# Two gated layers after a spectral convolution: two weight slices on four tiles first, two groups by VectorE, outputs in two buffers

## Chip, cores and metric

The kernel runs on 1 core of one Trainium2 chip. The metric is the device time of one execution in microseconds (us). Each time is the median of several executions. One execution taken by the hardware profiler gives the trace.

## What is computed

```
X = rfft(x, axis=1);  y = irfft(X * (filt_r + 1j*filt_i), n=3008, axis=1)   # x: 2 x 3008 x 256
t = y.reshape(6016, 256)
t = (sigmoid(t @ w_gate) * (t @ w_val)) @ w_out          # d_ff 1536
h = t @ w_in2
out = (h * sigmoid(1.702 * h)) @ w_out2                  # d_ff 2048
```

The MLP weights arrive as float64 and are decoded on the chip.

## The kernel before

**Precision.** Each f32 operand of a layer is split in a rounded high part (ScalarE) and a low part (a subtraction on VectorE or GpSimd), tiles with names ending in 0 and 1. `mm3` multiplies in three passes: lines 120, 121 and 122 are high x high, weight high x input low, weight low x input high.

**Convolution.** `Conv` does a DFT of length 3008 in two factors, as matmuls against tables, in 8 groups of 32 channels with two halves each (16 steps), for one batch entry at a time. Steps a0 to d0 are batch 0, run alone at the start; a1 to e1 are batch 1, run between matmuls of the first layer. The last step, `d0`, leaves times in PSUM; VectorE transposes them to `tt` (L235), and `store` writes them to DRAM (`yscr`), where `load_y` fetches a tile later. Only for the layer's first two tiles of batch 0 do results go straight to their input `yraw`: by DMA out of `tt` (L243) for groups 0 to 6, by a second transpose on VectorE (L304) for group 7.

**First layer.** 12 tiles of 512 or 480 tokens. A *unit* (`s12`) is one tile with one of the 12 slices (f) of 128 hidden channels: 12 front matmuls (gate and value, two halves c of the input channels) into two of four PSUM banks ps0 to ps3, then `gated` (sigmoid on ScalarE L389, multiply on VectorE, split), then 6 back matmuls into the tile's accumulators (`s12_back`; ps4, ps5 or ps6, ps7). Backs run two units late (`push`, depth 2). Tiles 0 and 1 go first, slice by slice in turn, because the weights are still being decoded: `load_raw` brings 512 KB of float64 words (SP queue), `decode_steps` makes f32 of them with five VectorE passes (L153, L158, L161, L164, L168), one ScalarE pass, and a split with the low half on GpSimd (L117). There are 18 such pieces in the order `job_w1(0)`, `job_w2(0)`, `job_w1(1)`, ...; `job_w1(f)` is the gate and value slice f (`wg`), `job_w2(f)` two output slices (`wo`). For these two tiles `gated` works in place in PSUM, with the low half on VectorE (L392 multiply, L117 low half). Then tiles 2 to 11 follow, 12 units each; 40 of the units carry the convolution of batch 1. Results go to DRAM (`xscr`).

**Second layer.** Tiles in six pairs, with a seven-product scheme (Strassen-Winograd) over blocks of 2 x 2: `combine_w` makes sums of weights, `combine_x` of inputs; they are cut into `chores` that the loop calls at fixed places. Here the order on all engines is that of the code. A pair has 8 sets of 45 matmuls; after a pair its two output tiles are copied out of PSUM (L756, L758) into `o`, one buffer, and stored.

**Order.** SP runs its DMAs in the order of the code throughout. In the convolution and the first layer a scheduler places the other engines' instructions at build time; each engine then runs its list in order.

## Time and profile before

| | us |
|---|---|
| median of 3 runs (lowest, highest) | 1220.15 (1218.12, 1223.8) |
| the profiled execution | 1219.74 |
| its span in the trace | 1217.8 |
| TensorE matmuls busy | 1169.5 |
| VectorE / ScalarE / GpSimd busy | 681.5 / 659.0 / 573.4 |

The trace has, for each instruction, its start, duration and what released it. PE is TensorE, PEld its weight loads, DVE VectorE, ACT ScalarE, POOL GpSimd, SP the queue of most DMAs. A matmul of 512 columns shows about 0.39 us from start to end, but the next one starts sooner; so matmuls are counted against time, and a full bar does not mean full speed. A clock of 1.00 is 2.4 GHz, 0.50 is 1.2 GHz.

### The profile page before, as it was taken

Reading aid. Unit: us, or ns where it says so; the run is one execution under the profiler, and the core shown is the slowest. Engines: PE = TensorE matmul, PEld = TensorE weight load, DVE = VectorE, ACT = ScalarE, POOL = GpSimd, SP = SyncE. Lnnn points to the kernel's source line nnn. Section 1 sums busy time; section 2 is a strip of 40 time slices with the busy share of each in tenths; the row PEclk is TensorE's granted clock in tenths of the full one; section 3 lists DMA queues with packets and bytes.
Section 4 is the critical chain, followed back from the end, with each engine's and each line's share of the span. In section 5 each row is a group of like instructions: output and inputs, shape, how many; then the busy total and the mean of one; then the engine's idle time right before and its main releaser. Section 6 shows DMA issues by size and latency. Waiting matters only on the chain.

```text
span 1217.8 us, 14310 instructions
## 1 busy us (share of the span) xinstructions
PE 1169.5 (96%) x5072; PEld 951.0 (78%) x5072; DVE 681.5 (56%) x1055; ACT 659.0 (54%) x1171; POOL 573.4 (47%) x456
## 2 busy tenths in 40 slices
PE   8869899999999999999999989999999999999998
PEld 3447688887878888888888867878888888788886
DVE  7889944565553552452744547645546556555443
ACT  5445544565653443343433446666666666666664
POOL 6622314666653542433433334545545555455453
PEclk9979999999999999999999999999999999999999
DMA  7444501222202121120210110020010010200000
GB/s 183 117 153 131 129 1 60 53 74 68 71 14 79 51 87 52 35 87 15 72 35 1 52 52 1 1 70 1 1 70 1 25 44 1 70 1 1 35 1 33
DMA packets 31351, 61.73 MB, mean 51 GB/s; under 512 B 3088, under 2 KB 10512, under 8 KB 31280
## 3 DMA queue, kind: packets, MB, share of 16 engines
q1 hardware_dynamic: 30992, 60.57, 16.6%
q8 instruction: 39, 0.64, 0.2%
q10 hardware_dynamic: 288, 0.26, 0.1%
q14 instruction: 32, 0.26, 0.1%
HBM read 42.20 MB, written 17.69 MB: 49 GB/s over the span
## 4 chain that ended last, share of the span: by engine, by line
PE 85%; DVE 8%; issue 3%; DMA 2%; ACT 1%; POOL 1%; SPq 0%; ACTq 0%; DVEq 0%; POOLq 0%
PE ps L120 28%; PE ps L122 28%; PE ps L121 28%; DMA out_dram<-o 1%; DVE m L161 1%; DVE c L164 1%; PE ps L257 1%; DVE m L158 1%; DVE m L168 1%; DVE g L117 1%; DVE ps L392 0%; DVE yp L495 0%; DMA f<-in_fd_dram 0%; DVE y L282 0%; DVE z L292 0%
## 5 line engine op out<-in xcount | busy, mean ns | idle before, releaser
L117 POOL TENSOR_TENSOR g<-sg,g 128x512 fp32r<-128x512 f32 (+1 forms) x216 | 282.2, 1311 | 396.1 <-ACT g L116 383.2
L120 PE MATMUL ps<-yp,wg 128*128 128x512 f32 (+1 forms) x576 | 225.4, 391 | 14.5 <-ACT yp L116 7.8
L121 PE MATMUL ps<-yp,wg 128*128 128x512 f32 (+1 forms) x576 | 224.2, 389 | 4.3 <-POOL yp L117 4.3
L122 PE MATMUL ps<-yp,wg 128*128 128x512 f32 (+1 forms) x576 | 223.6, 388 | 0.0
L116 ACT ACTIVATE g<-sg 128x512 fp32r<-128x512 f32 (+1 forms) x216 | 134.6, 623 | 123.2 <-DVE sg L395 111.1
L742 DVE TENSOR_TENSOR sg<-ps,sg 128x512 f32<-128x512 f32 (+1 forms) x192 | 130.0, 677 | 114.9 <-ACT sg L739 109.0
L739 ACT ACTIVATE sg<-ps 128x512 f32<-128x512 f32 (+1 forms) x192 | 113.2, 590 | 140.9 <-DVE ps L818 42.8
L117 POOL TENSOR_TENSOR wo<-sg,wo 128x512 fp32r<-128x512 f32 (+1 forms) x96 | 126.3, 1326 | 116.4 <-ACT wo L116 102.6
L395 DVE TENSOR_TENSOR sg<-ps,sg 128x512 f32<-128x512 f32 (+1 forms) x120 | 80.8, 674 | 158.0 <-PE ps L122 151.1
L120 PEld LDWEIGHTS ps<-yp,wg 128*128 128x128 f32 x576 | 109.0, 189 | 39.1 <-DVE g L117 9.9
L389 ACT ACTIVATE sg<-ps 128x512 f32<-128x512 f32 (+1 forms) x144 | 84.1, 584 | 89.6 <-POOL g L117 47.2
L121 PEld LDWEIGHTS ps<-yp,wg 128*128 128x128 f32 x576 | 109.0, 189 | 25.3 <-POOL yp L117 5.2
L122 PEld LDWEIGHTS ps<-yp,wg 128*128 128x128 f32 x576 | 108.9, 189 | 21.0
L122 PE MATMUL ps<-g,wo 128*128 128x512 f32 (+1 forms) x288 | 111.7, 388 | 0.0
L121 PE MATMUL ps<-g,wo 128*128 128x512 f32 (+1 forms) x288 | 111.6, 388 | 0.0
L120 PE MATMUL ps<-g,wo 128*128 128x512 f32 (+1 forms) x288 | 111.6, 388 | 0.0
L120 PE MATMUL ps<-g,wp 128*128 128x512 f32 (+1 forms) x192 | 74.8, 390 | 6.4 <-ACT o L756 6.4
L120 PE MATMUL ps<-wg,wi 128*128 128x512 f32 (+1 forms) x192 | 74.1, 386 | 0.8 <-DVE ps L822 0.8
L122 PE MATMUL ps<-g,wp 128*128 128x512 f32 (+1 forms) x192 | 74.3, 387 | 0.0
L121 PE MATMUL ps<-g,wp 128*128 128x512 f32 (+1 forms) x192 | 74.2, 387 | 0.0
L121 PE MATMUL ps<-wo,wp 128*128 128x512 f32 (+1 forms) x192 | 74.1, 386 | 0.0
L122 PE MATMUL ps<-wo,wp 128*128 128x512 f32 (+1 forms) x192 | 74.1, 386 | 0.0
(152 smaller groups left out, 2192.1 us busy)
## 6 DMA issues: line engine op xcount, KB each, us to landing
raw<-in_w_out_dram SPq DMA_DIRECT2D x14, 512.0 KB, 3.8
f<-in_fd_dram SPq DMA_DIRECT2D x16, 384.0 KB, 4.7
xscr<-x SPq DMA_DIRECT2D x12, 512.0 KB, 3.2
yraw<-xscr SPq DMA_DIRECT2D x12, 512.0 KB, 4.9
x<-in_xd_dram SPq DMA_DIRECT2D x15, 384.0 KB, 4.6
yscr<-tt SPq DMA_DIRECT2D x40, 128.0 KB, 2.2
yraw<-yscr SPq DMA_DIRECT2D x10, 512.0 KB, 5.4
raw<-in_w_in_dram SPq DMA_DIRECT2D x8, 512.0 KB, 3.6
```

Source lines behind the costliest of these rows:

```text
L116: nc.scalar.activation(out=dst_hi, in_=src, func=AF.Copy)
L117: lo_eng.tensor_sub(dst_lo, src, dst_hi.bitcast(F32))
L120: nc.tensor.matmul(out=o, lhsT=w[0], rhs=x[0], start=first, stop=False, **kw)
L121: nc.tensor.matmul(out=o, lhsT=w[0], rhs=x[1], start=False, stop=False, **kw)
L122: nc.tensor.matmul(out=o, lhsT=w[1], rhs=x[0], start=False, stop=last, **kw)
L158: nc.vector.tensor_scalar(m, hw, 0xFFFFF, 0x100000, op0=ALU.bitwise_and, op1=ALU.bitwise_or)
L161: nc.vector.scalar_tensor_tensor(out=f, in0=lw, scalar=2.0**-32, in1=m, op0=ALU.mult, op1=ALU.add)
L164: nc.vector.scalar_tensor_tensor(out=cu, in0=hw, scalar=0x80000000, in1=cu, op0=ALU.bitwise_and, op1=ALU.bitwise_or)
L389: nc.scalar.activation(out=sg[:, :n], in_=sig_src[:, :n], func=AF.Sigmoid, scale=scale)
L395: nc.vector.tensor_mul(sg[:, :n], val_src[:, :n], sg[:, :n])
L739: nc.scalar.activation(out=self.sg, in_=self.bank, func=AF.Sigmoid, scale=1.702)
L742: nc.vector.tensor_mul(self.sg, self.bank, self.sg)
```

## The change

1. **Convolution.** Groups 6 and 7 of batch 0 are transposed by VectorE straight into `yraw`; their DMAs out of `tt` fall away.
2. **First layer.** After slices 0 and 1 on tiles 0 and 1, slices 0 and 1 (`FK = 2`) run on tiles 2 and 3, too; then tiles 0 and 1 go on with slices 2 to 11, and later tiles 2 and 3 with slices 2 to 11 (10 units each). Since the accumulators are needed again, the partial sums of all four tiles are copied by ScalarE to new tiles `part` and stored in `xscr`; before the last back matmuls they are loaded again and added by VectorE in place of the copies. Tile 3's input is split once more later, after a second load.
3. **Staging.** Raw weights go alternately through two pools of one buffer each (before: one pool with three raw buffers).
4. **Loads of tile 6.** In tile 5 the load comes at slice 8 and the split at slice 10 (before 3 and 8).
5. **Second layer.** Output tiles use the two `yraw` buffers in place of the one `o`; for the last pair the first half's DMA is issued from ScalarE's queue. `combine_w` is cut in five chores (before three), and the loop calls a fourth chore per set.

```
-            if b == 0 and g < 7:
+            if b == 0 and g < 6:
...
-            if g == 7:
+            if g >= 6:
                 nc.vector.transpose(
-                    yraw[u][96:, 1, :].rearrange("p (n c) -> p n c", c=32), ...
+                    yraw[u][g % 4 * 32:g % 4 * 32 + 32, 1, :].rearrange("p (n c) -> p n c", c=32), ...
...
+    FK = 2
+    part = {}
...
-        acc = accs[1 if t == 1 else 0]
+        acc = accs[t % 2 if t < 2 or (t < 4 and f < FK) else 0]
...
+            if f == FC1 - 2 and t < 4:
+                part[t] = new_raw()
+                nc.sync.dma_start(out=part[t], in_=xscr[t]...)
...
+            if f == FK - 1 and t < 4:
+                part[t] = hold.tile([P, 2, 512], F32, name=f"part{t}")
+                for c in range(2):
+                    nc.scalar.copy(part[t][:, c, :n], acc[c][:, :n])
+                nc.sync.dma_start(out=xscr[t]..., in_=part[t])
+            elif last:
+                if t < 4:
+                    x2 = part[t]
+                    for c in range(2):
+                        nc.vector.tensor_add(x2[:, c, :n], x2[:, c, :n], acc[c][:, :n])
...
-    stage[0] = pools.enter_context(tc.tile_pool(name="st1", bufs=2))
-    nraw[0] = 3
-    for _ in range(3):
+    stage.append(right.enter_context(tc.tile_pool(name="st1", bufs=1, side="right")))
+    for _ in range(2):
         next_raw()
...
-    raw = load_y(2)
-    for f in range(1, FC1):
+    raw = [load_y(2), load_y(3)]
+    for t in range(2):
+        s12(t, 1, parts[t], in_place=True)
...
+    for f in range(FK):
+        for t in (2, 3):
+            s12(t, f, parts[t], in_place=True)
+            if raws:
+                decode()
+                next_raw()
+    for f in range(FK, FC1):
         for t in range(2):
             s12(t, f, parts[t], in_place=True)
             if raws and (t == 0 or f % 2 == 1):
...
-        for f in range(FC1):
+        for f in range(FK if t < 4 else 0, FC1):
...
+        return [
+            whole,
+            lambda: sums(0),
+            lambda: (hi(0), hi(1), sums(1)),
+            lambda: (lo(0), lo(1), hi(2), hi(3)),
+            lambda: (lo(2), lo(3)),
+        ]
...
-                if f == 3 and t > 2:
+                if f == (8 if t == 5 else 3):
                     raw = load_y(t + 1)
-                if f == 8:
+                if f == (10 if t == 5 else 8):
...
-                    outs[t] = work.tile([P, 2, 512], F32, tag="o", name="o", bufs=1)
+                    outs[t] = new_raw()
...
-                nc.sync.dma_start(out=out[...], in_=outs[t][:, c, :n])
+                (nc.scalar if t >= nt - 2 and c == 0 else nc.sync).dma_start(out=out[...], in_=o)
...
             bx.sig()
             back()
+            chore()
```

How the built programs stand, at three places. First VectorE, right after the last transposes of the convolution of batch 0. `ex`, `m`, `c` belong to decoding, `sg` and `g` to the gating of tiles 0 and 1 (PSUM banks ps1 and ps3). Before:

```order
L235 STREAM_TRANSPOSE tt_495<-ps7_78 96x512
L153 TENSOR_SCALAR ex_527<-raw_447 128x512
L158 TENSOR_SCALAR m_531<-raw_447 128x512
L161 SCALAR_TENSOR_TENSOR m_531<-raw_447,m_531 128x512
L164 SCALAR_TENSOR_TENSOR c_529<-raw_447,c_529 128x512
L153 TENSOR_SCALAR ex_553<-raw_449 128x512
L168 SCALAR_TENSOR_TENSOR m_531<-m_531,c_529 128x512
L158 TENSOR_SCALAR m_557<-raw_449 128x512
L164 SCALAR_TENSOR_TENSOR c_555<-raw_449,c_555 128x512
L161 SCALAR_TENSOR_TENSOR m_557<-raw_449,m_557 128x512
L153 TENSOR_SCALAR ex_594<-raw_452 128x512
L168 SCALAR_TENSOR_TENSOR m_557<-m_557,c_555 128x512
```

Now:

```order
L237 STREAM_TRANSPOSE tt_491<-ps7_78 96x512
L394 TENSOR_TENSOR ps1_72<-ps1_72,sg_521 128x512
L155 TENSOR_SCALAR ex_528<-raw_446 128x512
L160 TENSOR_SCALAR m_532<-raw_446 128x512
L394 TENSOR_TENSOR ps3_74<-ps3_74,sg_548 128x512
L117 TENSOR_TENSOR g1_524<-ps1_72,g0_523 128x512
L163 SCALAR_TENSOR_TENSOR m_532<-raw_446,m_532 128x512
L166 SCALAR_TENSOR_TENSOR c_530<-raw_446,c_530 128x512
L117 TENSOR_TENSOR g1_551<-ps3_74,g0_550 128x512
L170 SCALAR_TENSOR_TENSOR m_532<-m_532,c_530 128x512
L155 TENSOR_SCALAR ex_555<-raw_448 128x512
```

Three decodings stood ahead of the first gating multiply (the third is shown only in part); now both multiplies and both low halves (`g1`) are mixed with the first decoding.

TensorE at the same place: `wg` times `yp` is front, `wo` times `g` is back. Before, from the end of the first slice on:

```order
L122 MATMUL ps3_74<-yp0_124,wg1_82 128x512
L120 MATMUL ps0_71<-yp0_122,wg0_81 128x512
L121 MATMUL ps0_71<-yp1_123,wg0_81 128x512
L122 MATMUL ps0_71<-yp0_122,wg1_82 128x512
L120 MATMUL ps0_71<-yp0_122,wg0_81 128x512
L121 MATMUL ps0_71<-yp1_123,wg0_81 128x512
L122 MATMUL ps0_71<-yp0_122,wg1_82 128x512
```

Now:

```order
L122 MATMUL ps3_74<-yp0_124,wg1_82 128x512
L120 MATMUL ps4_75<-g0_523,wo0_83 128x512
L121 MATMUL ps4_75<-g1_524,wo0_83 128x512
L122 MATMUL ps4_75<-g0_523,wo1_84 128x512
L120 MATMUL ps5_76<-g0_523,wo0_83 128x512
L121 MATMUL ps5_76<-g1_524,wo0_83 128x512
L122 MATMUL ps5_76<-g0_523,wo1_84 128x512
L120 MATMUL ps0_71<-yp0_122,wg0_81 128x512
L121 MATMUL ps0_71<-yp1_123,wg0_81 128x512
```

The back of tile 0's first slice (it needs the first piece of `wo`) has moved ahead of the second slice's front matmuls.

Last VectorE in the second layer's first pair, between the multiply of one set and the first addition of the next (L807, now L852). `wv` and `wr` are sums of weights, the rows that write `wi1` and `yp1` their low halves. Before:

```order
L742 TENSOR_TENSOR sg_5575<-ps3_74,sg_5575 128x512
L495 TENSOR_TENSOR wi1_3086<-wr_5517,wi0_3085 128x128
L495 TENSOR_TENSOR yp1_5122<-wr_5517,yp0_5121 128x128
L495 TENSOR_TENSOR yp1_5503<-wr_5517,yp0_5502 128x128 x2
L742 TENSOR_TENSOR sg_5590<-ps0_71,sg_5590 128x512
L483 TENSOR_TENSOR wv_5592<-wi0_3085,wi1_3086 128x512
L484 TENSOR_TENSOR wr_5593<-wv_5592 128x128
L485 TENSOR_TENSOR wr_5593<-wr_5593,wv_5592 128x128
L486 TENSOR_TENSOR wr_5593<-wv_5592 128x128
L487 TENSOR_TENSOR wr_5593<-wv_5592,wr_5593 128x128
L807 TENSOR_TENSOR ps2_73<-ps2_73,s15_5512 128x512
```

Now:

```order
L783 TENSOR_TENSOR sg_5601<-ps3_74,sg_5601 128x512
L511 TENSOR_TENSOR wr_5549<-wv_5548 128x128
L512 TENSOR_TENSOR wr_5549<-wv_5548,wr_5549 128x128
L518 TENSOR_TENSOR wi1_3218<-wr_5549,wi0_3217 128x128
L518 TENSOR_TENSOR yp1_5154<-wr_5549,yp0_5153 128x128
L783 TENSOR_TENSOR sg_5616<-ps0_71,sg_5616 128x512
L518 TENSOR_TENSOR yp1_5535<-wr_5549,yp0_5534 128x128 x2
L852 TENSOR_TENSOR ps2_73<-ps2_73,s15_5544 128x512
```

The row `wv` and two of the sums have gone behind the addition or ahead of this piece.

## Rows read from the trace of the kernel before

**Rows 1.** The page, part 4: the ending chain, share of the span by engine.
```profile
PE 85%; DVE 8%; issue 3%; DMA 2%; ACT 1%; POOL 1%; SPq 0%; ACTq 0%; DVEq 0%; POOLq 0%
```

**Rows 2.** Waits of TensorE, whole span: releaser, us in total, times, longest.
```profile
PE ps L120 <- DVE g L117: 6.5, 6, 3.4
PE ps L120 <- ACT o L756: 6.4, 5, 1.3
PE ps L120 <- ACT s L812: 5.7, 2, 3.6
```

**Rows 3.** Stretches: busy us (instructions) of PE, PEld, DVE, ACT, POOL; granted clock, DMA.
```profile
75.20:78.80 3.60, 0.79 (x1) 0.29 (x1) 2.44 (x4) 3.00 (x4) 3.60 (x3) 0.50 0.66 224
78.80:84.90 6.10, 6.07 (x15) 4.83 (x16) 5.37 (x6) 2.16 (x4) 3.48 (x3) 0.52 0.48 145
84.90:113.90 29.00, 29.00 (x129) 23.99 (x128) 28.33 (x45) 15.75 (x28) 7.00 (x6) 1.00 0.35 115
113.90:147.00 33.10, 29.79 (x124) 22.46 (x123) 33.10 (x53) 15.73 (x27) 9.24 (x7) 1.00 0.51 138
147.00:160.00 13.00, 9.62 (x36) 7.45 (x35) 9.29 (x12) 9.41 (x16) 9.36 (x7) 0.87 0.07 14
```

**Rows 4.** Timeline after the first convolution: start, us, engine, line; [idle before, releaser].
```profile
65.44 1.16 SPq L243 DMA_DIRECT2D yraw<-tt  x2
...
66.60 1.57 DVE L304 STREAM_TRANSPOSE yraw<-ps 32x512 f32<-32x512 f32 x2 [0.59 <-PE ps L299]
...
74.71 2.85 POOL L117 TENSOR_TENSOR wo<-m,wo 128x512 fp32r<-128x512 f32 x1 [13.11 <-ACT wo L116]
...
75.20 0.79 PE L120 MATMUL ps<-yp,wg 128*128 128x512 f32 x1 [7.78 <-ACT yp L116]
...
78.83 0.80 PE L121 MATMUL ps<-yp,wg 128*128 128x512 f32 x1 [2.83 <-POOL yp L117]
...
83.68 0.63 PE L120 MATMUL ps<-yp,wg 128*128 128x512 f32 x1
```

**Rows 5.** Timeline of VectorE, first layer's first two tiles.
```profile
91.33 0.69 DVE L392 TENSOR_TENSOR ps<-ps,sg 128x512 f32<-128x512 f32 x1
...
103.29 1.73 DVE L161 SCALAR_TENSOR_TENSOR m<-raw,m 128x512 f32<-128x512 uint32 x1
...
146.83 0.69 DVE L392 TENSOR_TENSOR ps<-ps,sg 128x512 f32<-128x512 f32 x1
...
163.14 0.70 DVE L392 TENSOR_TENSOR ps<-ps,sg 128x512 f32<-128x512 f32 x1 [2.02 <-PE ps L122]
...
167.22 0.70 DVE L392 TENSOR_TENSOR ps<-ps,sg 128x512 f32<-128x512 f32 x1 [2.02 <-PE ps L122]
```

**Rows 6.** Timeline of TensorE, where decoding ends.
```profile
151.57 0.50 PE L120 MATMUL ps<-yp,wg 128*128 128x512 f32 x1 [3.38 <-DVE g L117]
```

**Rows 7.** Timeline of the second layer's first pair of tiles.
```profile
719.05 2.89 DVE L495 TENSOR_TENSOR yp<-wr,yp 128x128 fp32r<-128x128 f32 x3
...
723.50 1.24 DVE L485 TENSOR_TENSOR wr<-wr,wv 128x128 f32<-128x128 f32 x1
...
725.06 0.69 DVE L807 TENSOR_TENSOR ps<-ps,s 128x512 f32<-128x512 f32 x1
...
726.97 0.79 PE L120 MATMUL ps<-wg,yp 128*128 128x512 f32 x1 [3.64 <-ACT s L812]
```

**Rows 8.** Timelines of the first pair boundary and of the end.
```profile
809.22 0.58 ACT L756 COPY o<-ps 128x512 f32<-128x512 f32 x1 [1.40 <-DMA out_dram<-o]
...
809.86 0.50 PE L120 MATMUL ps<-g,wp 128*128 128x512 f32 x1 [1.31 <-ACT o L756]
...
1211.83 0.38 PE L122 MATMUL ps<-wo,wp 128*128 128x480 f32 x1
...
1213.73 0.66 DVE L758 COPY o<-ps 128x480 f32<-128x480 f32 x1 [2.13 <-DMA out_dram<-o]
```

**Rows 9.** The page, part 6: DMA issues of one kind, KB, median us to landing.
```profile
raw<-in_w_out_dram SPq DMA_DIRECT2D x14, 512.0 KB, 3.8
```

More of the change, by code (lines that the diff above doesn't have):

```diff
@@ L127 @@
     ebias = const.tile([P, 1], F32, name="ebias")
-    stage = [None]
-    nraw = [1]
+    stage = []
+    turn = [0]
     raws = []
@@ L133, in load_raw @@
         dst, srcs, shape = job
-        raw = stage[0].tile([P, 512, 2], U32, tag="raw", name="raw", bufs=nraw[0])
+        st = stage[turn[0] % len(stage)]
+        turn[0] += 1
+        raw = st.tile([P, 512, 2], U32, tag="raw", name="raw")
         at = 0
@@ L142, in load_raw @@
             at += n
-        raws.append((raw, dst, shape))
+        raws.append((raw, dst, shape, st))
     def decode(lo_eng=None):
@@ L149, in decode_steps @@
     def decode_steps(lo_eng=None):
-        raw, dst, shape = raws.pop(0)
+        raw, dst, shape, st = raws.pop(0)
         lw, hw = raw[:, :, 0], raw[:, :, 1]
-        ex = stage[0].tile([P, 512], U32, tag="ex", name="ex")
+        ex = st.tile([P, 512], U32, tag="ex", name="ex")
         nc.vector.tensor_single_scalar(ex, hw, 0x7FF00000, op=ALU.bitwise_and)
         yield
-        c = stage[0].tile([P, 512], I32, tag="c", name="c")
+        c = st.tile([P, 512], I32, tag="c", name="c")
         nc.scalar.activation(out=c, in_=ex, func=AF.Relu, bias=ebias, scale=8.0)
-        m = stage[0].tile([P, 512], U32, tag="m", name="m")
+        m = st.tile([P, 512], U32, tag="m", name="m")
         nc.vector.tensor_scalar(m, hw, 0xFFFFF, 0x100000, op0=ALU.bitwise_and, op1=ALU.bitwise_or)
@@ L430, in s12_mm @@
         mm3(o[:, :n], [w[:, f, v, c, :] for w in wg], [y[:, c, :n] for y in yp], c == 0, c == 1)
+    FK = 2
+    part = {}
     def s12_back(t, f, gp):
         n = tiles[t][3]
-        acc = accs[1 if t == 1 else 0]
+        acc = accs[t % 2 if t < 2 or (t < 4 and f < FK) else 0]
+        first, last = f == 0, f == FC1 - 1
+        if t < 4:
+            first, last = f in (0, FK), f in (FK - 1, FC1 - 1)
         def back():
+            if f == FC1 - 2 and t < 4:
+                part[t] = new_raw()
+                nc.sync.dma_start(out=part[t], in_=xscr[t].rearrange("(c p) n -> p c n", p=P))
             for c in range(2):
                 cs = slice(c * P, (c + 1) * P)
-                mm3(acc[c][:, :n], [w[:, f, cs] for w in wo], gp, f == 0, f == FC1 - 1)
-            if f == FC1 - 1:
-                x2 = work.tile([P, 2, 512], F32, tag="o", name="x2", bufs=1)
-                nc.scalar.copy(x2[:, 0, :n], acc[0][:, :n])
-                nc.vector.tensor_copy(x2[:, 1, :n], acc[1][:, :n])
+                mm3(acc[c][:, :n], [w[:, f, cs] for w in wo], gp, first, last)
+            if f == FK - 1 and t < 4:
+                part[t] = hold.tile([P, 2, 512], F32, name=f"part{t}")
+                for c in range(2):
+                    nc.scalar.copy(part[t][:, c, :n], acc[c][:, :n])
+                nc.sync.dma_start(out=xscr[t].rearrange("(c p) n -> p c n", p=P), in_=part[t])
+            elif last:
+                if t < 4:
+                    x2 = part[t]
+                    for c in range(2):
+                        nc.vector.tensor_add(x2[:, c, :n], x2[:, c, :n], acc[c][:, :n])
+                else:
+                    x2 = work.tile([P, 2, 512], F32, tag="o", name="x2", bufs=1)
+                    nc.scalar.copy(x2[:, 0, :n], acc[0][:, :n])
+                    nc.vector.tensor_copy(x2[:, 1, :n], acc[1][:, :n])
                 if n < 512:
@@ L541 @@
     conv = Conv(0, early.enter_context(tc.tile_pool(name="fx0", bufs=3)), ff0, fw0)
-    stage[0] = early.enter_context(tc.tile_pool(name="st0", bufs=1))
+    right = ExitStack()
+    stage.append(right.enter_context(tc.tile_pool(name="st0", bufs=1, side="right")))
     nc.scalar.dma_start(out=tabs[:, :256], in_=tab[:, :256])
@@ L606 @@
     split_y(1, yraw[1], parts[1], 1, nc.vector, slice(96, P))
+    pools.close()
+    pools = ExitStack()
+    hold = pools.enter_context(tc.tile_pool(name="hold", bufs=1))
     for t in range(2):
@@ L614 @@
         next_raw()
-    raw = load_y(2)
-    for f in range(1, FC1):
+    raw = [load_y(2), load_y(3)]
+    for t in range(2):
+        s12(t, 1, parts[t], in_place=True)
+    parts += [new_parts(), [hold.tile([P, 2, 512], F32R, name=f"yh{i}") for i in range(2)]]
+    for t in (2, 3):
+        for c in range(2):
+            split_y(t, raw[t - 2], parts[t], c)
+    for f in range(FK):
+        for t in (2, 3):
+            s12(t, f, parts[t], in_place=True)
+            if raws:
+                decode()
+                next_raw()
+    np_ = parts[2]
+    for f in range(FK, FC1):
         for t in range(2):
@@ L621 @@
                 next_raw()
-            if f == 2 and t == 0:
-                np_ = new_parts()
-                for c in range(2):
-                    split_y(2, raw, np_, c)
-                raw = load_y(3)
     while raws:
@@ L629 @@
     pools.close()
+    right.close()
+    stage.clear()
     pools = ExitStack()
@@ L684 @@
                     wp = [w34.tile([P, FC2, D], F32R, name=f"wp{i}") for i in range(2)]
-                    stage[0] = ctx.enter_context(tc.tile_pool(name="st2", bufs=1))
-                    nraw[0] = 1
+                    stage.append(ctx.enter_context(tc.tile_pool(name="st2", bufs=1)))
                     for i in range(0, FC2, 2):
```

36 lines of the change are left out of this document (20 added, 16 removed).

## The prediction

> **What bounds the kernel now.** I read the page first: the chain that ended last is TensorE for 85% of the span [rows 1], so only what makes TensorE stop, or run at its lower clock, can be won back. The waits of TensorE by releaser come next [rows 2]: three of the groups lie where the change works. VectorE's low half of the gated value (6.5 us in 6 waits) belongs to the first layer's first two tiles, the copy of an output tile (6.4 us in 5 waits) to the second layer's pair boundaries, the copy at L812 (5.7 us in 2) to its first pair. Two more waits are read in the stretch after the first convolution [rows 4]: 7.78 us until 75.20 for a high half and 2.83 us until 78.83 for a low half of the input.
>
> Then the stretches [rows 3], where the reader should set matmuls against time. From 84.9 to 113.9 us, 129 matmuls take 29.00 us, 0.225 each, though VectorE is already full. From 113.9 to 147.0 only 124 run in 33.1 us (27.9 at that pace), from 147.0 to 160.0 only 36 in 13.0 (8.1). These two lose 5.2 + 4.9 = 10.1 us. VectorE is why: while it decodes weights, its multiply of one unit (a pass of one weight slice over one tile, 12 + 6 matmuls) comes at 91.33 and, 11 units later, at 146.83, so 5.05 us per unit; without decoding the next two stand 4.08 apart [rows 5], which is TensorE's own pace. The last of these waits, 3.38 us, ends at 151.57 [rows 6].
>
> The profiled execution took 1219.74 us (span 1217.8), 0.4 under the median 1220.15. Savings are taken off it, and the 0.4 added back at the end.
>
> **The part after the first convolution.** Before, groups 4 to 6 of the convolution reach the tiles' second half of channels by DMA, the last issued at 65.44 [rows 4], and TensorE's next matmul waits until 75.20. Now groups 6 and 7 are written by VectorE. That adds two transposes of the kind that took 1.57 us for two [rows 4]; they stand ahead of the last convolution steps, so these end some 1 us later, near 69.0. ScalarE and VectorE then need two short passes each (about 0.65, estimated from the 0.69 of a multiply [rows 5]), and the 12 matmuls of the second half run at about 69 to 72 us instead of 75.20 to 83.68.
>
> Most of this is given back by the new order on VectorE. The two gating multiplies now stand ahead of the decoding of the next two weight pieces, and on TensorE the first six output matmuls ahead of the second slice. Counted from 71.7 us: two multiplies, two low halves and five steps of the first piece, about 0.6 apart, end at 76.6; ScalarE's high half and GpSimd's low half (0.6 and 1.3) make the output weights ready near 78.6. The second piece takes VectorE until about 80.2 (one step delayed by GpSimd) and is ready at 82.2. So the second slice starts at 82.3, against 83.68 before [rows 4], with six output matmuls behind it that before were still ahead. The wait of some 4 us before it drops the clock: after the 7.78 us wait the 6.1 us from 78.8 were run at 0.52, the 1.2 GHz level [rows 3]. I carry the same stretch over, until about 88. By 91.8 us TensorE has then done 48 matmuls of this layer, before 46. Worth **0.5 us**. Bounds: if GpSimd's pass again takes 2.85 us, as at 74.71 [rows 4], and pushes VectorE as much, 2.5 lost; if no clock is lost and nothing collides, 4.5 won.
>
> **The decode stretch.** Tiles 2 and 3 are taken in for the first two slices: four units more that need no new weights, so decoding gets 16.3 us more of TensorE work to hide behind (4 x 4.08 [rows 5]). These units come off the later stage, so the total of matmuls is unchanged. Price on VectorE: the 55.5 us between the two multiplies [rows 5] hold 11 units of two passes (2 x 0.69), two input splits (1.4) and 12 decodings, so one decoding is (55.5 - 15.2 - 1.4) / 12 = 3.24 us. In the new order 13 units in a row carry one decoding each: 1.38 + 3.24 = 4.62 us against 4.08, a lag of 0.54 per unit, 7.0 in all, behind a start about 0.9 late. The four front banks let TensorE run ahead by 30 matmuls (6.7 us) less the chain of four passes (2.6): 4.1 us. So 7.0 + 0.9 - 4.1 = 3.8 us of waits by this, and none if the passes pack as in the first 29 us of the stretch. I take 2.5 and keep 0 to 3.8: gain 10.1 - 2.5 = **7.6 us**.
>
> What comes with it: eight ScalarE copies, eight VectorE adds in place of four copies on each engine, four stores and four loads of 512 KB, and a second load of tile 3. ScalarE is busy 15.75 of 29.00 us in the densest stretch [rows 3]; the adds come when decoding is over. Zero, with this cover; without it each add would cost about 0.7. On SP the stores wait for ScalarE's copies, and the loads of raw weights stand behind them, with two raw buffers instead of three. A load of 512 KB lands after 3.8 us [rows 9], inside two decodings, so I count nothing; the fourth rival prices it. Tile 6 of the first layer is now loaded later in its predecessor; its split has about one unit of spare time, so 0 to 2 us.
>
> **Outputs through two buffers.** At each of five pair boundaries the second tile's copy waits for the first one's DMA (1.40 us at 809.22), TensorE 1.31 behind it [rows 8]. Two buffers take the wait away: **6.4 us** [rows 2]. They are shared with the inputs of the next combination, whose loads were queued behind these stores anyway. At the end the last copy starts at 1213.73 although the last matmul was issued at 1211.83 [rows 8] and takes 0.4: **1.5 us**. One output DMA of each last tile now goes from ScalarE's queue. The Trainium skill (DMA: Bandwidth & Descriptors, Issuing engines are not separate DMA queues) says that issuing from several engines saves only issue time. No run here shows that yet; by it this edit alone is worth under 1 us, and the sum does not count it.
>
> **Smaller combination steps.** In the first pair VectorE does four low halves (0.28 + 2.89 us), a multiply and five sums in a row before the addition at 725.06, and TensorE waits 3.64 us for it [rows 7]. Now at most two sums, a multiply and four short halves stand there: 2.4 us if GpSimd is quiet, 5.0 if each half costs what the three did, against 6.1. That takes 1.1 to 3.7 off the first wait and most off the second. Against it, two sums now precede another addition, 0.5 to 2.5 us. Range 0.7 to 7; I take **4 us**.
>
> **The sum.** 0.5 + 7.6 + 6.4 + 1.5 + 4 = 20.0: 1219.74 - 20.0 = 1199.7, and 1200 beside the median.
>
> **Rivals.** (1) VectorE stays the bound. At the old 5.05 us per unit over 13 units TensorE would lose 13 x 0.97 + 0.9 - 4.1 = 9.4 us and the stretch gives 0.7: 1207. For it: a step took 1.73 us at 103.29 where a multiply takes 0.69 [rows 5], while GpSimd worked. Against: this pace held 12 decodings and two splits in 11 units. The Trainium skill (SBUF — State Buffer, Who interferes with whom) calls the port that VectorE and GpSimd share an exclusive lock whose loser fully blocks; by that rule each unit pays such a meeting, which is this rival's time, and the trace agrees in the 1.04 us extra.
> (2) The start costs more: gating ahead of decoding, with GpSimd's 2.85 us pass [rows 4] met twice. The second slice starts 5 us later: 1205.
> (3) The start costs less: the clock holds and the copies collide little; with no lag in the stretch, 0.5 + 7.6 become 4.5 + 10.1 and the first pair gives 5: 1192.
> (4) Slower: SP's queue starves decoding. It decides when a decoding takes over 6.5 us: 13 x (6.5 - 4.08) + 0.9 - 4.1 = 28.3 us of waits against 22.5 at most won (20.0 + 2.5), 1226. With two buffers that needs 10 us from release to landing, against 3.8 [rows 9].
> (5) The second buffer does nothing, since the combination's inputs hold it: 6.4 less, 1206.
>
> **How the numbers follow.** Forecast 50%, (1) 17, (2) 11, (3) 13, (4) 4, (5) 5. 0.5% is 6.1 us, about what a measurement of this kernel tells from no change: faster than 1214 takes in all but (4) and bad sums of several, 0.93; within it 0.04; slower 0.03. The range takes in (1), (2), (3) and (5) with a little of their spread: 1191 to 1210.
>
> **What would show it.** Right: the first unit of tile 2 starts near 92 us; TensorE at 0.225 us per matmul from there past 150, with under 4 us of waits for the gated low half; no waits for the output copies; waits of the first pair under 3 us; VectorE's last copy right behind the last matmul. Wrong: VectorE waiting for raw weights, TensorE waiting for the first output weights beyond 79 us, or the clock at half past 90.

## The result, and the profile after

| | before | after |
|---|---|---|
| median (lowest, highest), us | 1221.89 (1218.12, 1223.8) | 1208.26 (1206.53, 1210.13) |
| ratio, 95% interval | | 0.9893 (0.9867 to 0.9919) |
| the profiled execution, its span | 1219.74, 1217.8 | 1206.53, 1204.7 |

Faster by 13.6 us; 20 were forecast. 1208 lies inside the range 1191 to 1210, near its upper end, 8 us above the forecast of 1200 and next to the time of the first rival, 1207.

Both programs issue 5072 matmuls, so the two traces can be set against each other by the start of the n-th one (counted from 0). What the difference (after less before) gains from one n to the next belongs to the stretch between. Two later executions with the same order on every engine, `after_again` and `split5` (below), stand beside it, since one execution has its own luck:

| matmuls | stretch | forecast | after | after_again | split5 |
|---|---|---|---|---|---|
| 0 to 48 | convolution, first groups | 0 | +2.4 | +1.8 | +0.1 |
| 48 to 176 | its end, and the start of layer 1 | -0.5 | -0.7 | +0.9 | -0.3 |
| 176 to 600 | decode stretch | -7.6 | -3.2 | -2.0 | -0.7 |
| 600 to 1600 | tiles 2 to 5, second convolution | 0 | +1.3 | +1.0 | -0.5 |
| 1600 to 2880 | rest of layer 1 | 0 | 0 | 0 | 0 |
| 2880 to 3040 | first pair of layer 2 | -4 | -4.3 | -4.4 | -4.4 |
| 3040 to 5071 | pair boundaries | -6.4 | -6.4 | -6.5 | -6.3 |
| behind the last matmul | end | -1.5 | -2.1 | -2.1 | -2.1 |
| sum | | -20.0 | -13.1 | -11.2 | -14.2 |

The second layer came as forecast in sum. In the profiled execution 7 us are missing: 4.4 in the decode stretch, 2.4 in the first groups of the convolution and 1.3 in tiles 2 to 5, less 1.1 that came on top in the other rows.

Waits of TensorE in the changed kernel (answering [rows 2]; releaser, us in total, times, longest):

```profile
PE ps L120 <- DVE g L117: 5.5, 6, 2.0
...
PE ps L120 <- DVE y L342: 2.7, 1, 2.7
PE ps L120 <- DVE ps L867: 2.2, 1, 2.2
...
PE ps L120 <- ACT s L857: 1.1, 1, 1.1
```

No wait for an output copy is left (6.4 before), and the first pair's 5.7 became 2.2 + 1.1. The wait for the gated low half only shrank from 6.5 to 5.5. The matmuls of some stretches (length, TensorE busy and count, granted clock, DMA share, GB/s):

```profile
80.00:100.00 20.00, 18.71 (x63) 0.76 0.30 95
100.00:120.00 20.00, 20.00 (x90) 1.00 0.61 193
120.00:140.00 20.00, 18.89 (x84) 1.00 0.46 149
140.00:160.00 20.00, 16.05 (x67) 1.00 0.44 137
160.00:180.00 20.00, 19.60 (x87) 1.00 0.42 101
```

TensorE runs 0.222 us per matmul only until 120; the loss begins later than before [rows 3], but it comes. The timeline of VectorE and SP shows why (start, us, engine, line; idle before and releaser in brackets):

```profile
98.92 0.68 DVE L170 SCALAR_TENSOR_TENSOR m<-m,c 128x512 f32<-128x512 f32 x1
...
101.16 0.70 DVE L394 TENSOR_TENSOR ps<-ps,sg 128x512 f32<-128x512 f32 x1 [0.80 <-ACT sg L391]
102.85 0.69 DVE L117 TENSOR_TENSOR g<-ps,g 128x512 fp32r<-128x512 f32 x1 [0.99 <-ACT g L116]
105.39 0.43 DVE L155 TENSOR_SCALAR ex<-raw 128x512 uint32<-128x512 uint32 x1 [1.85 <-DMA raw<-in_w_val_dram]
...
128.70 1.43 DVE L155 TENSOR_SCALAR ex<-raw 128x512 uint32<-128x512 uint32 x1 [0.88 <-DMA raw<-in_w_out_dram]
```
```profile
100.14 0.36 SPq L455 DMA_DIRECT2D xscr<-part  x1
100.60 0.41 SPq L140 DMA_DIRECT2D raw<-in_w_gate_dram  x1
101.06 0.87 SPq L140 DMA_DIRECT2D raw<-in_w_val_dram  x1
```

From 99.6 to 105.4 VectorE decodes nothing. In its list only the gating of two units stands there, for which it waits 0.80 and 0.99 us, and then raw weights are missing for 1.85 us more. After that it is full until 165, apart from 0.88 us before 128.70. The second thing to see is what GpSimd's low half of a decoded piece does to a VectorE step that begins beside it:

```profile
134.69 1.35 POOL L117 TENSOR_TENSOR wo<-m,wo 128x512 fp32r<-128x512 f32 x1 [4.83 <-ACT wo L116]
...
152.46 1.29 POOL L117 TENSOR_TENSOR wg<-m,wg 128x512 fp32r<-128x512 f32 x1 [3.77 <-ACT wg L116]
```
```profile
134.79 0.69 DVE L394 TENSOR_TENSOR ps<-ps,sg 128x512 f32<-128x512 f32 x1
...
152.57 1.72 DVE L163 SCALAR_TENSOR_TENSOR m<-raw,m 128x512 f32<-128x512 uint32 x1
```

The step at L163 takes 0.68 us alone; begun just behind GpSimd's pass it takes 1.72 and ends half a microsecond after that pass (153.75). The multiply L394, which reads PSUM, takes its 0.69 in the same place. Steps with one input are held, too: L155 at 128.70 takes 1.43 us in place of 0.42, GpSimd's pass having begun at 128.56. From 105 to 165 us twelve steps are held in this way, for 10.9 us in all.

### The profile page after: what moved, and what is told of

Same layout as the page of the kernel before. It is cut to its first block, busy times and chain, and to the rows that moved or that the text cites. A ratio compares the mean times of both kernels' runs of the same rounds, so it can differ in the third digit from the quotient of the medians.

```text
span 1204.7 us, 14326 instructions
## 1 busy us (share of the span) xinstructions
PE 1170.2 (97%) x5072; PEld 949.1 (79%) x5072; DVE 694.9 (58%) x1067; ACT 661.9 (55%) x1177; POOL 570.4 (47%) x452
## 4 chain that ended last, share of the span: by engine, by line
PE 87%; DVE 8%; issue 2%; DMA 2%; ACT 1%; POOL 0%; SPq 0%; DVEq 0%; ACTq 0%
PE ps L120 28%; PE ps L122 28%; PE ps L121 28%; DVE c L166 1%; DVE m L163 1%; DVE ps L394 1%; DVE m L170 1%; PE ps L259 1%; DVE m L160 1%; DVE g L117 1%; DVE y L284 0%; DVE ex L155 0%; DMA raw<-in_w_out_dram 0%; DVE z L294 0%; DVE a L261 0%
## 5 line engine op out<-in xcount | busy, mean ns | idle before, releaser
L117 POOL TENSOR_TENSOR g<-sg,g 128x512 fp32r<-128x512 f32 (+1 forms) x212 | 277.6, 1314 | 374.6 <-ACT g L116 353.9
L120 PE MATMUL ps<-yp,wg 128*128 128x512 f32 (+1 forms) x568 | 221.6, 391 | 6.1 <-DVE g L117 5.5
L121 PE MATMUL ps<-yp,wg 128*128 128x512 f32 (+1 forms) x568 | 220.6, 388 | 1.8 <-POOL yp L117 1.5
L122 PE MATMUL ps<-yp,wg 128*128 128x512 f32 (+1 forms) x568 | 220.3, 388 | 0.6 <-POOL wg L117 0.6
L116 ACT ACTIVATE g<-sg 128x512 fp32r<-128x512 f32 (+1 forms) x212 | 132.0, 623 | 111.5 <-DVE sg L397 100.9
L117 POOL TENSOR_TENSOR wo<-sg,wo 128x512 fp32r<-128x512 f32 (+1 forms) x96 | 130.0, 1364 | 111.4 <-ACT wo L116 91.6
L783 DVE TENSOR_TENSOR sg<-ps,sg 128x512 f32<-128x512 f32 (+1 forms) x192 | 129.9, 677 | 89.9 <-ACT sg L780 82.5
L397 DVE TENSOR_TENSOR sg<-ps,sg 128x512 f32<-128x512 f32 (+1 forms) x116 | 77.9, 671 | 150.7 <-PE ps L122 143.5
L120 PEld LDWEIGHTS ps<-yp,wg 128*128 128x128 f32 x568 | 107.3, 189 | 30.4 <-DVE g L117 8.3
L121 PEld LDWEIGHTS ps<-yp,wg 128*128 128x128 f32 x568 | 107.3, 189 | 22.3 <-POOL yp L117 1.8
L122 PEld LDWEIGHTS ps<-yp,wg 128*128 128x128 f32 x568 | 107.2, 189 | 21.9 <-POOL wg L117 1.4
L120 PE MATMUL ps<-wg,wi 128*128 128x512 f32 (+1 forms) x192 | 74.1, 386 | 2.2 <-DVE ps L867 2.2
L120 PE MATMUL ps<-g,wp 128*128 128x512 f32 (+1 forms) x192 | 74.3, 387 | 0.0
L122 PE MATMUL ps<-wo,wp 128*128 128x512 f32 (+1 forms) x192 | 74.1, 386 | 0.0
L121 PE MATMUL ps<-wo,wp 128*128 128x512 f32 (+1 forms) x192 | 74.1, 386 | 0.0
L121 PE MATMUL ps<-wg,wi 128*128 128x512 f32 (+1 forms) x192 | 74.1, 386 | 0.0
L120 PE MATMUL ps<-wo,wp 128*128 128x512 f32 (+1 forms) x192 | 74.1, 386 | 0.0
```

The costliest lines, as they stand in the source:

```text
L116: nc.scalar.activation(out=dst_hi, in_=src, func=AF.Copy)
L117: lo_eng.tensor_sub(dst_lo, src, dst_hi.bitcast(F32))
L120: nc.tensor.matmul(out=o, lhsT=w[0], rhs=x[0], start=first, stop=False, **kw)
L121: nc.tensor.matmul(out=o, lhsT=w[0], rhs=x[1], start=False, stop=False, **kw)
L122: nc.tensor.matmul(out=o, lhsT=w[1], rhs=x[0], start=False, stop=last, **kw)
L397: nc.vector.tensor_mul(sg[:, :n], val_src[:, :n], sg[:, :n])
```

## The experiments

The theories on the decode stretch: **A**, VectorE is starved of raw weights (by the stores in SP's queue, or by having two buffers); **B**, each decoding is dear because VectorE is held once per piece by GpSimd. Two more on tile 5: **D**, the input split beside GpSimd; **E**, the shifted convolution steps. All ratios are to the kernel before, timed beside each kernel on the same chip. "Stretch" is matmuls 176 to 600 by the count above.

### part_act

```
-                nc.sync.dma_start(out=xscr[t]..., in_=part[t])
+                nc.scalar.dma_start(out=xscr[t]..., in_=part[t])
```

> The changed kernel with one edit: the four stores of partial sums are issued from ScalarE's queue, so that on SP no load of raw weights stands behind a store that waits for ScalarE's copies. Theory A (starved decoding): in the changed kernel SP's next raw load waited behind the first such store from about 91.5 until 100.6 us, and VectorE decoded nothing between 99.5 and 105.4; this time is missing later, where TensorE waits 5.5 us in six waits for the gated low half. It expects VectorE to decode through that stretch, the six waits to shrink to 2 us or less in total, and about 3.5 us less than the changed kernel (1204 to 1205). Theory B (each decoding is dear because VectorE meets GpSimd's low half once per piece, 1.0 to 1.1 us each): the waits stay at 4 us or more and the time within 1.5 us of the changed kernel (1207 to 1209).

Measured: 1209.84 us, 0.9884 (0.9868 to 0.99); stretch -1.0. VectorE did decode through 99 to 105, and then starved later, so the stores in SP's queue are not what keeps TensorE waiting:

```profile
104.83 0.37 SPq L140 DMA_DIRECT2D raw<-in_w_out_dram  x1
```
```profile
104.13 0.68 DVE L166 SCALAR_TENSOR_TENSOR c<-raw,c 128x512 uint32<-128x512 uint32 x1
...
109.69 0.43 DVE L155 TENSOR_SCALAR ex<-raw 128x512 uint32<-128x512 uint32 x1 [2.95 <-DMA raw<-in_w_out_dram]
```
```profile
PE ps L120 <- DVE g L117: 6.7, 9, 1.1
```

The load goes out the moment the buffer is free (its last reader, L166, ends at 104.81) and VectorE gets on 4.9 us later. VectorE waited 4.9 us for raw weights in this stretch, 2.7 before the edit, and TensorE 6.7 us for the gated low half, 5.5 before.

### low_dve

```
             if raws:
-                decode()
+                decode(nc.vector)
...
             if raws and (t == 0 or f % 2 == 1):
-                decode()
+                decode(nc.vector)
...
     while raws:
-        decode()
+        decode(nc.vector)
```

> The changed kernel with one edit: from the first unit of tiles 2 and 3 on, the low half of each decoded weight piece is made by VectorE instead of GpSimd. GpSimd then does nothing in this stretch that VectorE could meet. Theory B (meetings): 13 pieces lose 1.04 us each and gain a pass of 0.60, so VectorE's price per unit falls from 4.97 (59.6 us for 12 units between 105.4 and 165.0) to 1.20 + 2.46 + 0.60 = 4.26, the waits of TensorE for the gated low half fall from 5.5 to under 1 us, and the time by 4 to 5 us (1203 to 1204). No pass of 0.42 us or 0.69 us should show 1.4 to 1.8 us any more. Theory A alone (the 5 us without raw weights is the whole loss): the gap of VectorE before 105.4 us stays, the price per unit matters little, and TensorE still waits 3 us or more. Rival C: the extra pass waits for ScalarE's high half in VectorE's order, and the price per unit stays near 5 us: no change.

Measured: 1198.51 us, 0.9792 (0.9778 to 0.9806); stretch -10.7, the whole loss of the kernel before. No wait for the gated low half is left. From 106.25 to 163.00 us a unit on VectorE, from one multiply to the next, is 4.05 us on average, TensorE's pace, with a sixth pass in each decoding. One of 3.88 us:

```profile
122.40 0.69 DVE L394 TENSOR_TENSOR ps<-ps,sg 128x512 f32<-128x512 f32 x1
123.00 0.42 DVE L160 TENSOR_SCALAR m<-raw 128x512 uint32<-128x512 uint32 x1
123.33 0.69 DVE L117 TENSOR_TENSOR wg<-m,wg 128x512 fp32r<-128x512 f32 x1
123.94 0.69 DVE L117 TENSOR_TENSOR g<-ps,g 128x512 fp32r<-128x512 f32 x1
124.54 0.68 DVE L163 SCALAR_TENSOR_TENSOR m<-raw,m 128x512 f32<-128x512 uint32 x1
125.14 0.69 DVE L166 SCALAR_TENSOR_TENSOR c<-raw,c 128x512 uint32<-128x512 uint32 x1
125.77 0.43 DVE L155 TENSOR_SCALAR ex<-raw 128x512 uint32<-128x512 uint32 x1
126.28 0.70 DVE L394 TENSOR_TENSOR ps<-ps,sg 128x512 f32<-128x512 f32 x1
```

From 105 us on no VectorE step of a decoding takes 1.2 to 1.8 us any more, as B said. Its price was 4 to 5 us; by the stretch 7.5 to 10 came back (three executions of the changed kernel, 0.7 to 3.2), by the ratios 6 to 12. The holds alone don't make this up: 10.9 us of them against 13 passes of 0.60 are 3.1 us of VectorE. The edit also gave VectorE a new list. In it the 13 decodings stand beside 14 units; in the changed kernel they stand beside 12 (106.80 to 165.07). How much each of the two is worth, no run separates. A costs nothing visible any more: VectorE still waits 0.9 us for raw weights, and TensorE does not notice.

### low_dve_idle

```
-        split(*dst, f..., lo_eng or nc.gpsimd)
+        split(*dst, f..., lo_eng or nc.gpsimd); lo_eng and len(stage) > 1 and nc.gpsimd.tensor_sub(st.tile([P, 512], F32, tag="idle", name="idle")..., dst[0].bitcast(F32), dst[0].bitcast(F32))
```

> low_dve with one addition: where the changed kernel had GpSimd make the low half of a decoded piece, GpSimd now subtracts the high half from itself into a tile that nobody reads (15 passes of 128x512). No result waits for these passes and no buffer of the decoding is held by them; the order of all other engines is that of low_dve. Theory B (VectorE is held while GpSimd's pass runs): single VectorE passes show 1.4 to 1.8 us again, the price per unit rises by 1.0 to 1.1 us to 5.1 to 5.4, the waits of TensorE for the gated low half come back with 8 us or more, and the time rises to 1206 to 1210. Rival G (what low_dve won is the earlier release of the decoding's buffers, or the shorter way to the finished weights): VectorE's passes stay short, no waits, 1198 to 1200.

Measured: 1205.06 us, 0.9856 (0.9835 to 0.9876); stretch -3.6, 7.1 us less than low_dve's. The profiled execution is the slowest of five, which go from 1200.54 to 1206.77. Fifteen passes whose result nobody reads make steps long again (0.93 to 1.54 us in place of 0.69), so G alone falls. Each held a step by less than expected (0.25 to 0.85 us; these passes take GpSimd 1.04 when nothing holds them), and the price per unit rose to 4.3 (106.50 to 167.32, 14 units), not 5.1. TensorE's loss came as one wait at the end, with the clock down behind it:

```profile
173.32 0.79 PE L120 MATMUL ps<-yp,wg 128*128 128x512 f32 x1 [3.29 <-DVE g L117]
```
```profile
170.00:175.00 5.00, 1.72 (x5) 0.72 0.19 47
175.00:180.00 5.00, 5.00 (x15) 0.60 0.00 0
```

This wait has a second cause. The low half that releases TensorE waited for ScalarE, and ScalarE stood for a load of the second convolution that is next in its list:

```profile
171.09 0.83 ACT L231 COPY f<-f 64x768 f32<-64x768 f32 x1 [3.02 <-DMA f<-in_fd_dram]
```
```profile
172.57 0.69 DVE L117 TENSOR_TENSOR g<-ps,g 128x512 fp32r<-128x512 f32 x1 [3.78 <-ACT g L116]
```

In low_dve ScalarE stands at the same place for 2.52 us and TensorE does not wait. So the holds used up TensorE's lead (14 units at 4.34 us in place of 4.05, an estimate of 4.1 us), and the load then showed. The 7.1 us are the price of both and of the clock, not of the passes alone.

The holding goes both ways: GpSimd's pass of 1.04 us takes 2.83 where VectorE's passes came first.

```profile
129.39 2.83 POOL L173 TENSOR_TENSOR idle<-wg 128x512 f32<-128x512 f32 x1 [3.50 <-ACT wg L116]
133.58 1.04 POOL L173 TENSOR_TENSOR idle<-wo 128x512 f32<-128x512 f32 x1 [1.36 <-ACT wo L116]
```

### raw3

```
-        st = stage[turn[0] % len(stage)]
+        st = stage[min(turn[0] % 3, len(stage) - 1)]
...
-        raw = st.tile([P, 512, 2], U32, tag="raw", name="raw")
+        raw = st.tile([P, 512, 2], U32, tag="raw", name="raw", bufs=2 if len(stage) > 1 and st is stage[1] else 1)
...
-    for _ in range(2):
+    for _ in range(3):
         next_raw()
```

> The changed kernel with three raw buffers instead of two (one piece more is loaded ahead); the stores stay in SP's queue. Theory A with the buffers as its cause: the third piece covers the time in which SP's queue stands behind the stores; VectorE's pause before 105.4 us goes, the waits for the gated low half fall from 5.5 to 2.5 us or less, the time by 3 us (1205). Theory A with the queue as its cause: the pause shrinks by one decoding (3.5 us of about 5) at most, 1 to 3 us. Theory B: no change in the waits (5 us or more), 1207 to 1209.

Measured: 1202.02 us, 0.9822 (0.9809 to 0.9835); stretch -5.9, TensorE's wait for the gated low half 2.8 us:

```profile
PE ps L120 <- DVE g L117: 2.8, 6, 0.9
```

The stretch is 3 to 5 us better than the changed kernel's; the median is 2.5 us under that of split5, which has the changed kernel's order and ran beside it. That does not show the buffers as the cause. VectorE waits for raw weights as long as before, 3.0 us against 2.7:

```profile
DVE ex L155 <- DMA raw<-in_w_val_dram: 2.1, 1, 2.1
...
DVE ex L155 <- DMA raw<-in_w_out_dram: 0.9, 1, 0.9
```

The scheduler orders every engine anew when the third buffer is there. In this order GpSimd holds five VectorE steps from 105 to 165 us, for 4.0 us in all, where it held twelve for 10.9; VectorE in its turn waits 2.9 us for GpSimd's low halves to free a buffer. Fewer meetings explain the gain as well as the buffer does, so theory A stays open.

### b_low

The kernel before, with `decode(nc.vector)` in the first layer's loops in place of `decode()`.

> The kernel before with the low halves of the decoded weights made by VectorE instead of GpSimd, and nothing else. In the old order 11 units stand beside 12 decodings and two splits. Theory B: 12 x (2.46 + 0.60) + 11 x 1.20 + 1.2 = 51.1 us of VectorE where the trace of before took 55.5, so the stretch loses about 5 to 6 us instead of 10.1, and the time falls by 4 to 5 us (0.996). If the four-tile order and the passes off GpSimd were worth the same thing twice, this edit alone would bring the 10 us that low_dve shows in its stretch; if the four-tile order alone were enough, the changed kernel would have shown it. Rival G (buffers): no change, the kernel before has three raw buffers already.

Measured: 1213.41 us, 0.9929 (0.9915 to 0.9944); stretch -10.1, twice what was expected, and this is all that is left of TensorE's wait for the gated low half:

```profile
PE ps L120 <- DVE g L117: 0.2, 1, 0.2
```

My 51.1 us kept 12 decodings in 11 units; with the edit the scheduler spreads them over 14 units, from a multiply at 90.33 to one at 147.22, 4.06 us each. So with the low halves off GpSimd the old order hides the decoding as well as the new one (10.1 against 10.7): the two edits are worth the same 10 us, once.

### split5, after_again

```
-                if f == (10 if t == 5 else 8):
-                    nxt = new_parts()
-                    for c in range(2):
-                        split_y(t + 1, raw, nxt, c)
+                if f == (10 if t == 5 else 8):
+                    nxt = new_parts()
+                if t == 4 and f in (8, 9):
+                    split_y(t + 1, raw, nxt, f - 8)
+                elif t != 4 and f == (10 if t == 5 else 8):
+                    for c in range(2):
+                        split_y(t + 1, raw, nxt, c)
```

> The changed kernel with one edit: the two halves of the input split of tile 5 (made during tile 4) are made in two successive units instead of both in one. In the changed kernel both stand in a row at 329.03 us and take 4.76 us together, while GpSimd is busy, the next step of the convolution comes late, TensorE waits 2.73 us at 334.32 and its clock is at 0.91 in that stretch of 20 us. By the count of matmuls this place cost 2.3 us against the kernel before. Theory D (the split in a row is the cause): the wait of 2.73 us falls under 1 us, the clock stays at 1.00 there, and the time falls by 2 to 4 us (1204 to 1206). Rival E (the convolution's steps fall on other units than before, and it is they that wait): a wait of 2 us or more stays within 30 us of that place, and the time stays within 1 us of the changed kernel.

Measured: 1204.5 us, 0.9844 (0.9829 to 0.9859). The edit moved nothing: the scheduler places the split where its data are there, and both halves stand in a row as before, 4.78 us for the two. So it says nothing on D or E and serves as a repeat of the changed kernel. `after_again` is that kernel, unaltered:

> The changed kernel once more, unaltered, beside the kernels of this batch. split5 turned out to have the order of the changed kernel on every engine (its edit moved nothing), yet gave 0.9844 of the kernel before where the changed kernel gave 0.9893, and its trace took 2.3 us less for the first 48 matmuls and 2.7 us more around 170 us. Expected if these are chances of an execution: a ratio between 0.983 and 0.991, the first 48 matmuls done between 28.0 and 31.6 us, and waits of TensorE for the gated low half between 5 and 8 us. Expected if split5 is really another kernel: the ratio of the changed kernel again, 0.987 or more.

Measured: 1208.36 us, 0.9875 (0.9855 to 0.9894). Three sets of runs of one order thus gained 13, 15 and 19 us. Over the 14 traces of all kernels matmul 48 starts between 28.02 and 31.59 us. The profiled execution of the kernel before, from which the sum was taken off, has the 28.02: the luckiest of them.

The decode stretch differs by chance, too. In after_again and split5 TensorE stops twice more at its end, at the 494th and 500th matmul (0.46 and 0.54 us, 1.59 and 0.55 us), when ScalarE stands for loads of the second convolution. In the profiled execution of the changed kernel these loads had landed.

### split5_pool

```
-                        split_y(t + 1, raw, nxt, c)
+                        split_y(t + 1, raw, nxt, c, nc.gpsimd if t == 4 else nc.vector)
```

> The changed kernel with both low halves of the input split of tile 5 on GpSimd instead of VectorE. In the changed kernel VectorE takes 4.76 us for the two (1.28 without company), the time that three passes of GpSimd take there (1.30 + 1.22 + 0.99 us), and the convolution's step behind them makes TensorE wait 2.4 to 2.7 us in every trace so far, with the clock down behind it in some. Theory D: the wait for that step falls under 0.7 us, 2 to 4 us less at this place by the count of matmuls. Rival F: GpSimd is the late one now (two passes of 1.2 us ahead of the next gated low half), and TensorE waits 2 us or more for GpSimd there instead.

Measured: 1204.75 us, 0.9857 (0.984 to 0.9874). In the changed kernel:

```profile
329.29 1.30 POOL L117 TENSOR_TENSOR zp<-z,zp 128x512 fp32r<-128x512 f32 x1
330.54 1.22 POOL L117 TENSOR_TENSOR g<-sg,g 128x480 fp32r<-128x480 f32 x1
331.71 0.99 POOL L343 TENSOR_TENSOR v<-v,f 128x384 f32<-128x384 f32 x1
```
```profile
329.03 4.76 DVE L117 TENSOR_TENSOR yp<-yraw,yp 128x480 fp32r<-128x480 f32 x2 [0.43 <-ACT yp L116]
333.72 0.55 DVE L342 TENSOR_TENSOR y<-ps,f 128x384 f32<-128x384 f32 x1
```
```profile
334.32 0.48 PE L120 MATMUL ps<-zp,tab 128*96 128x512 f32 x1 [2.73 <-DVE y L342]
```

VectorE's two passes end when GpSimd's three have. With the passes on GpSimd, TensorE's wait for L342 is gone, and the stretch from matmul 1120 to 1280 costs 1.1 us less than before, where the changed kernel's cost 2.3 more. Theory D holds; F did not come. The time, 0.9857, lies between those of the changed kernel (0.9893, 0.9875, 0.9844), so the gain is seen in the trace alone.

### low_all, best_a

`low_all` is low_dve with `decode(nc.vector)` for the first two pieces, too.

> low_dve with the same edit on the two pieces decoded first after the convolution as well: all low halves of the first layer's weights by VectorE. In the changed kernel these two passes take GpSimd 1.79 us each at 80.00 and 83.80, and each holds one VectorE step for 1.76 us instead of 0.69. Theory B (a meeting costs VectorE the time of GpSimd's pass): two passes of 0.60 replace two delays of 1.07, and the second slice waits for a pass of 0.69 instead of 1.79; the second slice starts about 1.5 to 2 us earlier against the last matmul of the convolution, and the time is 1 to 2 us under low_dve, 1196 to 1198. Rival: the start is set by the order of decoding alone, no change against low_dve within 0.7 us.

Measured: 1194.77 us, 0.9774 (0.9755 to 0.9792), 3.7 us under low_dve's median, on another chip; by the ratios it is 2.2 us, and the intervals overlap. From matmul 48 to 176 it is 1.8 us better than before, low_dve 0.9 worse: as expected, with a part that may be chance.

> low_all and split5_pool together: all low halves of the first layer's weights by VectorE, both low halves of tile 5's input split by GpSimd. If the two add up: no waits for the gated low half, none for the convolution's step in tile 4, and 2 to 3 us under low_all: 1191 to 1194, 0.975 to 0.976 of the kernel before.

Measured: 1193.05 us, 0.9766 (0.9749 to 0.9783), the fastest here. Beside low_all the difference is within the intervals; in its trace the wait in tile 4 is 0.2 us.

### b_outs

```
-                    outs[t] = work.tile([P, 2, 512], F32, tag="o", name="o", bufs=1)
+                    outs[t] = new_raw()
```

> The kernel before with one part of the change alone: output tiles in the two yraw buffers instead of the one o (all their DMAs still from SP's queue). The prediction's term: 6.4 us at five pair boundaries and 1.5 us at the end, 7.9 together: 0.9935 of the kernel before. The changed kernel's trace gave 1.4 us at each of five boundaries and 2.1 us at the end. Rival 5 of the prediction (the second buffer does nothing, since the inputs of the next combination hold it): under 2 us. If ScalarE's queue made the gain at the end, the end here stays as before, and 6.5 to 7 us remain.

Measured: 1212.55 us, 0.9921 (0.9904 to 0.9938). No wait for an output copy; by the count of matmuls 7.5 us at the five boundaries (1.5 each) and 2.0 at the end, 9.5 together, by the median 10.5. Forecast: 7.9. With all DMAs on SP's queue the end is 2.0 better, in the changed kernel 2.1: ScalarE's queue brings 0.1. That agrees with the Trainium skill (DMA: Bandwidth & Descriptors, Issuing engines are not separate DMA queues), which leaves such an edit only issue time.

### conv7

```
-            if b == 0 and g < 6:
+            if b == 0 and g < 7:
...
-            if g >= 6:
+            if g == 7:
```

> The changed kernel with its convolution as before: group 6 reaches the second half of the channels by DMA again, only group 7 by VectorE. By the prediction's step for the start, the wait of 7.8 us for that DMA comes back, VectorE decodes the first two pieces inside it, and the second slice starts where it did before, 16.9 us after the last matmul of the convolution (66.83 to 83.68); the changed kernel's trace has 13.6 us (70.20 to 83.77). Counted at the 176th matmul against the kernel before, the start then costs between 1.5 us more and 1.5 us less than the changed kernel's (which was 0.7 to 1.0 us better than before from the 48th to the 176th matmul). Rival: the convolution's edit is what makes the start better, then this kernel is 3 us slower than the changed one.

Measured: 1205.17 us, 0.9864 (0.9846 to 0.9883). From matmul 48 to 176 it is 1.3 us better than before, to 200 only 0.1; the changed kernel's three executions are between 0.7 better and 1.0 worse by 200. The wait for the DMA is back (7.26 us), the one for the first output weights is gone:

```profile
77.97 0.80 PE L120 MATMUL ps<-yp,wg 128*128 128x512 f32 x1 [7.26 <-ACT yp L116]
```

Beside the rest of the change the convolution's edit is worth nothing that can be told from chance: VectorE has to decode two pieces here, and TensorE waits for one thing or the other.

## Why the prediction was right or wrong

**The start (0.5): right in kind.** Three executions gave 0.7, -0.9 and 0.3, so 0.5 can't be told from nothing. The second half's matmuls begin at 71.39 instead of 75.20, TensorE waits 5.0 us for the first output weights at 79.97, the clock is down again (0.76 over 80 to 100, above), and the second slice's weights are there at 85.64:

```profile
71.39 0.73 PE L120 MATMUL ps<-yp,wg 128*128 128x512 f32 x2 [0.60 <-ACT yp L116]
...
79.97 0.80 PE L120 MATMUL ps<-g,wo 128*128 128x512 f32 x1 [5.01 <-ACT wo L116]
...
85.64 0.80 PE L122 MATMUL ps<-yp,wg 128*128 128x512 f32 x1 [0.64 <-POOL wg L117]
```

These lie 2.4 us late as the whole execution does. That the wait would only change its name was the forecast's point, and conv7 confirms it.

**The decode stretch (7.6): wrong, 3.2 came, and 0.7 to 2.0 in the repeats.** The price of a decoding was right: from 110.77 to 165.07, 11 units with 12 decodings took 54.3 us, less 0.9 idle and 11 x 1.38, is 3.2 each (3.24 forecast). The lag was mis-sized: 7.0 + 0.9 = 7.9 us in the forecast. From the multiply at 90.22 to the one at 165.07 there are 16 units in 74.85 us, where TensorE's pace of 4.08 gives 65.3, so the lag is 9.6. Less the lead of 4.1 that is 5.5 us by the forecast's own sum, as much as TensorE waited.

The step that failed, as far as is known, is the zero for the raw loads: "inside two decodings, so I count nothing". VectorE waited 2.7 us for them (1.85 and 0.88). Without these the lag would be 6.8 us and the waits 2.7, near the 2.5 taken; that is an estimate, and no run takes the wait away alone. With two buffers a buffer is held until the fourth step of its own piece, spread between the passes of the units, and was in use again 4.9 us after that in part_act. The fourth rival had the mechanism, but counted only landing time, not how long a piece holds its buffer; and it blamed SP's queue, whose relief in part_act brought nothing.

The first rival has the time: 1207, with 0.7 us from this stretch. Its mechanism was there, too, in the price of 3.2 itself: five passes alone fit in 2.5, and GpSimd holds one step per piece, by 0.9 us on average (10.9 us in twelve). I took that as given; it was the part that could be removed, as low_dve and b_low show, where the order changed with it. So the measured time lies in the range because the range took in this rival, and not because the sum held. The Trainium skill's rule cited there (SBUF — State Buffer, Who interferes with whom) lets a VectorE instruction contend with GpSimd's reads when both its inputs are in SBUF, and not when one is in PSUM; the rows of L163 and L394 above agree. The held L155 has a single input and is not covered by this.

**Tile 6 (0 to 2): the cost was at tile 5.** No term of the sum names it. The kernel before waits at the same place:

```profile
341.16 0.49 PE L120 MATMUL ps<-zp,tab 128*96 128x512 f32 x1 [2.13 <-DVE y L340]
```

In the changed kernel both halves of the split stand in a row, and the wait is 2.4 to 2.7 us. From matmul 1120 to 1280 that is 0.45 us more than before by the wait alone, and 2 to 2.3 where the clock falls behind it. So most of this loss is the clock's, and chance. Whether the partial sums, which share the input buffers, brought the two halves together, no run shows.

**The first convolution (0): chance.** The sum was taken from the luckiest opening of 14; the others are 1.6 us slower on average. Against a typical execution the gain is that much larger.

**Right:** output buffers (6.4 forecast; 7.5 at the boundaries, of which 1.1 is lost again in steps of 0.1 to 0.2 us elsewhere in the second layer, so that the sum of 6.4 fits by luck), the end (1.5; 2.1), the smaller steps (4; 4.3, the two waits 2.2 and 1.1 us, a little over the 3 named). The end's last copy stands right behind the last matmul:

```profile
1200.82 0.38 PE L122 MATMUL ps<-wo,wp 128*128 128x480 f32 x1
...
1201.23 0.66 DVE L801 COPY yraw<-ps 128x480 f32<-128x480 f32 x1 [0.65 <-PE ps L122]
```

Of the signs of being wrong, "VectorE waiting for raw weights" showed. TensorE also waited for the first output weights beyond 79 us, to 79.97, but the whole execution was 2.4 us late. Of the signs of being right, the pace of 0.225 us past 150 and the waits under 4 us for the gated low half failed.

## What to carry to other kernels

Before a new order is built to hide work on a full engine, look at the longest rows of a repeated step against its shortest: a step of 0.68 us that takes 1.72 once per round names a neighbour. Moving the neighbour's pass onto the full engine itself (0.6 us for 0.9 held), with the order that the scheduler then made, gave the whole 10 us that the four-tile order sought, and in the old order just as much. An edit that makes the scheduler place instructions anew tests the new order along with the edit: count units and held steps before naming a cause. A staging buffer's turn is the time that its piece holds it plus the time to fill it; with two of them, count both. Take a sum off several executions, not off one.
